# Transformer block on one core: the last four x tiles prepared later, two weight-sum sets moved into the first MLP product, rounds of h's turn every 80 steps

## The chip, the cores and the metric

The kernel runs on one core of one Trainium2 chip. The metric is the device time of one execution in microseconds (us). Lower is better. A run of the kernel also leaves a profile: one execution taken by the hardware profiler, with the records of TensorE (PE, with its weight loads PEld), VectorE (DVE), ScalarE (ACT), GpSimd (POOL), and of SyncE (SP), which issues most of the DMAs.

## The reference

One block: layer norm, an attention with a linear kernel (Hedgehog feature map), a product with `wo`, a residual; then layer norm, an MLP with ReLU, a residual. All in fp32, S = 2048 rows, D = 1024, 32 heads of 32, Dff = 3584.

```python
qkv = layernorm(x) @ wqkv                      # three parts, 32 heads of 32
pq, pk = q @ w_phi, k @ w_phi                  # per head, 32 x 32
phi_q = concat(softmax(pq), softmax(-pq)); phi_k likewise
kv = phi_k^T v;  z = sum of phi_k over the rows
o = (phi_q kv) / (phi_q z + 1e-6)
h = x + o @ wo
out = h + relu(layernorm(h) @ w1) @ w2
```

## The kernel before

**The products.** Each fp32 matrix is split in a high half (rounded to the TensorE type fp32r) and a low half (the rest), and each block of 128 x 128 by 512 takes three matmuls, high x high, high x low and low x high (lines 181, 182 and 183). Such a group of three is a *step*, and the whole kernel is written as a list of steps. A step's place in the list sets the order of instructions on TensorE. Items of eight steps (a tile of 128 rows by a slab of weights) make the projections, items of four steps make the two MLP products.

**The stages, in steps.** K and V for rows 0 to 1023 in four slabs of eight row tiles (steps 0 to 255), Q for these rows in two slabs (256 to 383), then K and V (384 to 639) and Q (640 to 767) for rows 1024 to 2047, the attention, the product with `wo`, the first MLP product (from program step 1024, called `up0`; it starts at 804 us and ends at 1342 us) and the second (to the end). Both MLP products use a scheme of seven instead of eight block products, numbered 1 to 7 and taken in the order 1, 5, 6, 2, 7, 3, 4, so sums of blocks of the weights and of the normalised h are formed beforehand. The first product runs twice over 14 chunks of Dff, once for rows 0 to 1023 (b = 0) and once for the others (b = 1, from 1071 us).

**Everything else is put beside the steps by hand.** `when(step, f, args)` puts a call of `f` behind the matmuls of that step. The calls issue instructions on DVE, ACT, POOL and SP in that order; each engine runs its own instructions in order, and waits in a queue where an operand or a buffer is not there yet. SP issues nearly all loads and stores, in the order of the program, so a load or store that has to wait holds up all DMAs behind it.

**Weights.** `Units.advance`, called behind every step, takes the blocks of weights in the order of their use: it issues the load of a raw block (line 215 and others; six buffers named `raw`) as soon as one of them is free, and a few steps ahead of use it splits the block, the high half by a copy on ACT (line 124), the low half by a subtraction on DVE or POOL (line 128), into a ring of ten buffers named `w`. A raw block's buffer comes free when its low half is done.

**Folded weights.** The feature map's matrix `w_phi` is multiplied into the Q and K weights on the chip. `wt_load` (line 320) loads rows of the transposed weights, `fold_part` (line 335, on TensorE, 64 small matmuls in the group of a fold) multiplies them into the banks, `fold_turn` (line 355, on DVE) transposes the result, `fold_store` (SP) writes it to DRAM, from where it comes back as raw blocks of the K and Q weights (`wpk`, `wpq`). Folds 1 to 7 stand at items 3, 9, 13, 17, 21, 25 and 29.

**The x tiles.** x has 16 tiles of 128 rows. Each of tiles 1 to 6 has steps of its own in `X_STEPS` (load, statistics, power, normalisation, two halves of the transposition). Tiles 0 to 7 go the straight way: load, statistics on DVE (line 221), power on POOL, normalisation on ACT (line 244), transposition on TensorE (line 288) and split. Tiles 8 to 15 are needed only from item 48 on. `X_EARLY` gives each of them a load (line 215), statistics and a normalisation (`xn_norm`, two calls on ACT, two steps apart), after which `xn_store` writes the result to DRAM. Later `xn_load` (line 262) fetches it, 88 to 64 steps ahead (tiles 8 to 11, at steps 241, 257, 273 and 289) or 36 steps ahead (tiles 12 to 15) of the place that `turn` names for its transposition on DVE. The loads of x tiles and of normalised tiles, among others, share the two buffers named `xin` of the pool `lnp`.

**Weight sums.** The sums of blocks of w1 and w2 for the MLP products are made in 56 *sets*, one after another: `t_load` (0.5 MB), four `t_sum` on POOL (line 420) and `t_store` (0.5 MB), written to DRAM and read from there in the MLP stages. `places` is the list of the steps at which they start: the first are the 21 *far* sets in the K and V slabs of the first half, then sets in the Q items and in the second half, and 14 in the first MLP product, from `up0 + 440`, every 25 steps.

**h's turn.** The normalised second half of h is prepared for the first MLP product's second pass in four rounds during its first pass. A round is the list `TURNS`, relative to its start: two reads of h, statistics, two loads of h in another order, normalisation by ACT, two transpositions by DVE (steps 47 and 51), sums on DVE and POOL (52 to 54, line 888), followed by seven stores (`turn_store`, steps 56 to 62). Four rounds start at `up0 + 25 + 84 * i`. Afterwards `h_load` (line 916) fetches each of the seven combinations in two halves, `h_high` (line 924, ACT) makes its high half and `h_low` (line 928, DVE) its low half, in the buffers `hT`, each in its place behind the last product of the first pass that uses the buffer. For b = 0 the low half stands two steps behind the high half for the first four combinations (j < 4) and five steps for the others.

**Beside the first MLP product** `UP_BESIDE` takes each finished bank: `up_take` on ACT (line 957 among them), `up_sum` on DVE (line 954) and so on.

Of the kernel before, what the change touches and what calls it, by code (L numbers as in the profile page):

```python
# [25 lines left out]
NP = NC // 2  # L26
# [113 lines left out]
def kernel(  # L140
# [47 lines left out]
    def do(n, k, f, *args):  # L188
        at[n, k].append((f, args))
# [847 lines left out]
    def item(gen, *args, keys):  # L1037
        items.append((gen, args + (keys,)))
        steps.extend((k,) for k in keys)
        return len(items) - 1  # L1040
# [11 lines left out]
    for b, tiles in enumerate(groups):  # L1052
        for hf in range(2):

            pairs = b == 0 and hf == 0
            for j in range(0, 4, 2 if pairs else 1):
# [3 lines left out]
                for half in range(2):  # L1060
                    n = item(wo_pair, tiles[j:j + 2], hf, half, keys=[("wo", hf, 4 * half + k // 2) for k in range(8)])
# [18 lines left out]
    def x_part(t):  # L1080
        return [x[t * P:(t + 1) * P, :]]
# [6 lines left out]
    def when(step, f, *args):  # L1088

        if step < 8 * first_up:  # L1090
            do(step // 8, step % 8, f, *args)
        else:
            do(first_up + (step - 8 * first_up) // 4, step % 4, f, *args)


    X_STEPS = {1: (None, None, None, None, 5, 7), 2: (None, 6, 8, 10, 12, 13), 3: (None, 10, 11, 14, 18, 20),
               4: (9, 19, 20, 24, 27, 28), 5: (15, 25, 26, 29, 35, 38), 6: (25, 33, 35, 37, 41, 44)}
    X_EARLY = ((48, 74, 86), (64, 84, 98), (88, 102, 112), (100, 115, 138), (116, 140, 154), (142, 158, 170),
               (158, 174, 203), (174, 204, 218))
    for t in range(1, NT):  # L1100
        n = t - 1 if t < HT else q_n[1, t - HT] + 1
        turn = 8 * n + 1
# [2 lines left out]
        else:  # L1105

            load_, stats, norm = X_EARLY[t - HT]
            when(load_, ln_load, ("s", t), x_part(t))
# [22 lines left out]
    for p, n in zip(range(1, 8), (3, 9, 13, 17, 21, 25, 29)):  # L1131
        step = 8 * n + (4 if p > 1 else 7)
# [82 lines left out]
    for u in range(32):  # L1215
        start = 8 * (a0 + u) if u >= 8 else 8 * (last_kv + 4) + 19 * u // 2
        slack = 6 if u < 5 else 0
        if u % 2:
            places = (-8 if u < 12 else -1, 6, 10, 13, 16, 19, 25 if u < 16 else 23)
            when(start + 30 + slack, at_num, u - 1)  # L1220
            when(start + 32 + slack, at_low, u - 1)
        elif u < 16:
            places = (-8 if u < 12 else -1, 6, 10, 13, 16, 19, 25)
        else:
            places = (6, 12, 17, 19, 21, 23, 29)
# [28 lines left out]
    up0 = 8 * first_up  # L1254
    for i in range(4):
        for stage in (0, 1, 2, 3, 9, 4, 5, 6, 7, 8):
            when(wo0 + 64 + 40 * i + LN2[i % 2][stage], ln_pair, 0, i, stage)
        for step, *what in TURNS:
            when(up0 + 25 + 84 * i + step, turn_pair, i, *what)
        for j in range(7):  # L1260
            when(wo0 + 64 + 40 * i + LN2[i % 2][10] + j // 2, ln_store, 0, i, j)
            when(up0 + 25 + 84 * i + 56 + j, turn_store, i, j)
    assert wo_n[8, 0] + 10 < first_up

    def up_step(b, p, m):

        return up0 + 4 * (up_n[b, p, m] + 1 - first_up)

    for j, m in enumerate(UP):

        for g in range(2):
            step = up0 + (8 * j + (-62, -32)[g] if j < 4 else 6 * (j - 4) + 10 + 2 * g)
            high = up0 + (8 * j + (-48, -19)[g] if j < 4 else 6 * (j - 4) + 20 + 2 * g)
            when(step, h_load, 0, m, g)
            when(high, h_high, m, g)
            when(high + (2 if j < 4 else 5), h_low, m, g)
            step = up_step(0, NP - 1, m) + 3 * j
            when(step + 3 * g, h_load, 1, m, g)
            when(step + 18 + 4 * g, h_high, m, g)
            when(step + 21 + 4 * g, h_low, m, g)  # L1280
# [8 lines left out]


    sets = [(w, p, j) for w in (1, 2) for p in range(NP) for j in range(2)]
    places = [64 * q + step for q in range(4) for step in (-9, -1, 7, 15, 23, 31) if 64 * q + step > 9]
    far_sets = len(places)
    places += [264, 274, 284, 294, 314, 364, 374]
    slabs = [8 * kv_n[1, q, HT] for q in range(4)]
    places += sorted([slab + step for slab in slabs for step in (8, 20, 32)] + [slab - 3 for slab in slabs[1:3]])
    places += [up0 + 440 + 25 * n for n in range(14)]
    for n, (step, (w, p, j)) in enumerate(zip(places, sets, strict=True)):
        far = n < far_sets
        when(step, t_load, w, p, j, lnp if step > up0 else fp if far and n % 4 > 1 else tsp)  # L1300
# [4 lines left out]
    for b in range(2):  # L1305
        for m in DOWN:
            n = down_n[b, m, NP - 1] + 1
# [164 lines left out]
```

## Time and profile before

| | |
|---|---|
| time of the runs, median of 3 | 1879.9 us (1879.06 to 1880.86) |
| the profiled execution, its own time | 1880.66 us |
| its span in the profile | 1878.9 us |
| mean granted TensorE clock | 0.998 |
| busy: PE, PEld | 99%, 81% of the span |
| busy: DVE, ACT, POOL | 57%, 40%, 53% |
| DMA traffic | 441.64 MB, mean 235 GB/s |

"Busy" is the time in which an engine executes; the time between two instructions of it counts as idle, and the profile names the instruction on another engine (or the transfer) that ended that idle time. A time of a group of instructions ("L181 PE MATMUL mm<-w") is for the source line 181 of the kernel, with the tile that is written and the tiles that are read. In the rows of a timeline the first number is the start in us from the start of the span, the second the duration, then the engine (SPq is SP's queue of DMAs), the line, the operation, the tiles and, in brackets, how long the engine stood idle just before and for what. The 1.8 us between the profiled execution's own time and its span lie outside the span.

### The profile page before, as it was taken

The page shows a single profiled execution, that of the slowest core. Times are in us where ns is not written, and L with a number is a line of the kernel's source. Part 1 is how long each engine was busy: PE and PEld are TensorE (multiplying, and loading weights), DVE is VectorE, ACT ScalarE, POOL GpSimd, SP SyncE. Part 2 cuts the span into 40 slices and gives each one's busy share as a digit, 9 for nine tenths or more (in the row PEclk, how much of TensorE's full clock was granted, in tenths as well). Part 3 has the DMA queues.
Part 4 walks back from the last instruction along what each step waited for, and adds up shares of the span by engine and source line. Part 5 has one row for each costly group of instructions (what it writes and reads, how often), then busy time and mean ns, then how long its engine had stood idle before and what let it go on. Part 6 is the DMA issues. An engine that isn't in the chain of part 4 may idle for free.

```text
span 1878.9 us, 31761 instructions
## 1 busy us (share of the span) xinstructions
PE 1861.3 (99%) x11502; PEld 1527.8 (81%) x11502; DVE 1074.5 (57%) x1714; ACT 747.1 (40%) x1272; POOL 996.0 (53%) x956
## 2 busy tenths in 40 slices
PE   9999999999999999999999999999999999999999
PEld 7777888888887888888888878888888888888887
DVE  7877789677889676465554674444433333343333
ACT  5443334222233122355454554444444444444442
POOL 4767756678745888233332334435444444444443
PEclk9999999999999999999999999999999999999999
DMA  6799877445465666898687997877877677767775
GB/s 215 245 308 327 291 243 241 131 149 175 135 224 184 206 213 215 266 292 294 214 286 247 297 316 240 264 249 259 274 237 216 205 227 240 236 215 219 216 214 178
DMA packets 320492, 441.64 MB, mean 235 GB/s; under 512 B 28112, under 2 KB 182736, under 8 KB 320336
## 3 DMA queue, kind: packets, MB, share of 16 engines
q1 hardware_dynamic: 291168, 398.69, 66.4%
q10 hardware_dynamic: 29168, 40.93, 6.6%
q8 instruction: 90, 1.47, 0.3%
q14 instruction: 66, 0.54, 0.1%
HBM read 297.96 MB, written 141.57 MB: 234 GB/s over the span
## 4 chain that ended last, share of the span: by engine, by line
PE 88%; DMA 5%; DVE 2%; SPq 1%; issue 1%; ACT 1%; POOL 1%; DVEq 0%; ACTq 0%; POOLq 0%
PE mm L181 22%; PE mm L182 22%; PE mm L183 22%; PE ac L183 3%; PE ac L182 3%; PE ac L181 3%; PE tp L181 2%; PE tp L183 2%; PE tp L182 2%; DMA hT<-hs 1%; PE tp L720 1%; PE ac L533 1%; PE ac L720 1%; DMA raw<-in_w_dram 1%; PE tp L288 1%
## 5 line engine op out<-in xcount | busy, mean ns | idle before, releaser
L128 POOL TENSOR_TENSOR w<-raw,w 128x512 fp32r<-128x512 f32 x353 | 476.5, 1352 | 641.7 <-ACT w L124 619.6
L124 ACT ACTIVATE w<-raw 128x512 fp32r<-128x512 f32 x686 | 408.9, 626 | 485.0 <-PE mm L183 221.1
L128 DVE TENSOR_TENSOR w<-raw,w 128x512 fp32r<-128x512 f32 x333 | 279.4, 840 | 508.8 <-ACT w L124 503.0
L181 PE MATMUL mm<-w,xT 128*128 128x512 f32 x752 | 298.3, 397 | 2.9 <-ACT w L124 2.9
L182 PE MATMUL mm<-w,xT 128*128 128x512 f32 x752 | 293.4, 390 | 0.5 <-POOL w L128 0.2
L183 PE MATMUL mm<-w,xT 128*128 128x512 f32 x752 | 292.8, 389 | 0.0
L182 PE MATMUL mm<-hT,w 128*128 128x512 f32 x672 | 261.8, 390 | 2.8 <-DVE hT L928 2.8
L181 PE MATMUL mm<-hT,w 128*128 128x512 f32 x672 | 261.6, 389 | 0.7 <-DVE c L954 0.7
L183 PE MATMUL mm<-hT,w 128*128 128x512 f32 x672 | 261.4, 389 | 0.0
L420 POOL TENSOR_TENSOR b<-b 128x256 f32<-128x256 f32 x168 | 133.4, 794 | 78.5 <-DMA b<-in_w_dram 70.0
L181 PEld LDWEIGHTS mm<-w,xT 128*128 128x128 f32 x752 | 141.3, 188 | 35.1 <-ACT w L124 3.3
L182 PEld LDWEIGHTS mm<-w,xT 128*128 128x128 f32 x752 | 141.4, 188 | 31.0 <-POOL w L128 1.1
L183 PEld LDWEIGHTS mm<-w,xT 128*128 128x128 f32 x752 | 141.3, 188 | 29.8
L181 PE MATMUL mm<-w 128*128 128x512 f32 x392 | 152.5, 389 | 0.0
L182 PE MATMUL mm<-w 128*128 128x512 f32 x392 | 152.5, 389 | 0.0
L183 PE MATMUL mm<-w 128*128 128x512 f32 x392 | 152.5, 389 | 0.0
L182 PEld LDWEIGHTS mm<-hT,w 128*128 128x128 f32 x672 | 126.1, 188 | 30.2 <-DVE hT L928 4.1
L181 PEld LDWEIGHTS mm<-hT,w 128*128 128x128 f32 x672 | 126.1, 188 | 27.4 <-DVE c L954 1.1
L183 PEld LDWEIGHTS mm<-hT,w 128*128 128x128 f32 x672 | 126.2, 188 | 25.9
L522 POOL TENSOR_TENSOR zacc<-zacc,kphi 128x512 f32<-128x512 f32 x60 | 82.7, 1378 | 7.0 <-DVE kphi L514 7.0
L181 PEld LDWEIGHTS mm<-w 128*128 128x128 f32 x392 | 73.6, 188 | 15.3
L183 PEld LDWEIGHTS mm<-w 128*128 128x128 f32 x392 | 73.6, 188 | 15.3
(200 smaller groups left out, 3181.0 us busy)
## 6 DMA issues: line engine op xcount, KB each, us to landing
raw<-t SPq DMA_DIRECT2D x224, 256.0 KB, 4.3
raw<-ad SPq DMA_DIRECT2D x196, 256.0 KB, 3.0
raw<-in_w_dram SPq DMA_DIRECT2D x168, 256.0 KB, 3.4
ad<-c SPq DMA_DIRECT2D x112, 256.0 KB, 4.2
b<-in_w_dram SPq DMA_DIRECT2D x42, 512.0 KB, 5.6
t<-b SPq DMA_DIRECT2D x42, 512.0 KB, 3.9
ad<-s SPq DMA_DIRECT2D x84, 256.0 KB, 4.7
ed<-qe ACTq DMA_DIRECT2D x32, 512.0 KB, 4.3
```

Of the source, the lines that this page charges most:

```text
L124: nc.scalar.activation(w[:, 0, :], raw[1], AF.Copy)
L128: eng.tensor_tensor(out=w[:, 1, :], in0=raw[1], in1=w[:, 0, :].bitcast(F32), op=ALU.subtract)
L181: pe.matmul(ps, a_hi, b_hi, start=first, stop=False, skip_group_check=more)
L182: pe.matmul(ps, a_hi, b_lo, start=False, stop=False, skip_group_check=more)
L183: pe.matmul(ps, a_lo, b_hi, start=False, stop=last, skip_group_check=more)
L288: pe.transpose(pt[:, k, :], xn[:, (4 * j + k) * P:(4 * j + k + 1) * P], ident)
L420: pool.tensor_tensor(out=tsum[j, *out], in0=tsum[j, *a], in1=tsum[j, *b], op=ALU.subtract)
L522: pool.tensor_tensor(out=zacc[s], in0=zacc[s], in1=phi_of[key], op=ALU.add)
L533: pe.matmul(kv_ps[s][g][32 * i:32 * (i + 1), 0:64], vt[:, 32 * h:32 * (h + 1)], phi[:, 64 * h:64 * (h + 1)], start=first, stop=last)
L720: pe.matmul(banks[g][32 * c:32 * (c + 1), r * P:(r + 1) * P], kvL[rows, 4 * q + 2 * sd + h // 4, 32 * (h % 4):32 * (h % 4 + 1)], phT[rows, ...
```

## The change

It edits six lists of steps, and no instruction's shape or kind.

- **x tile 6.** Statistics, power and normalisation at steps 30, 33 and 36, before at 33, 35 and 37.
- **x tiles 12 to 15, early pass.** The loads at steps 140, 168, 206 and 232 (before 116, 142, 158 and 174), the statistics and the normalisation, and with it the store, 14 to 36 steps behind their loads as listed below.
- **Far sets.** `places` now leaves out steps 119 and 183. The number of far sets falls from 21 to 19. As the sets are made in a fixed order, each set takes the next place in the list.
- **Sets in the first MLP product.** 16 of them, every 22 steps, from the same step; before 14, every 25 steps.
- **h's turn.** Rounds every 80 steps, with their stores; before every 84.
- **h_low for j >= 4 (b = 0)** stands three steps behind `h_high`, before five. **h_load for b = 1** stands `5 * j // 2` steps behind the last product of the first pass, before `3 * j`; `h_high` and `h_low` move with it.

```diff
-               4: (9, 19, 20, 24, 27, 28), 5: (15, 25, 26, 29, 35, 38), 6: (25, 33, 35, 37, 41, 44)}
-    X_EARLY = ((48, 74, 86), (64, 84, 98), (88, 102, 112), (100, 115, 138), (116, 140, 154), (142, 158, 170),
-               (158, 174, 203), (174, 204, 218))
+               4: (9, 19, 20, 24, 27, 28), 5: (15, 25, 26, 29, 35, 38), 6: (25, 30, 33, 36, 41, 44)}
+    X_EARLY = ((48, 74, 86), (64, 84, 98), (88, 102, 112), (100, 115, 138), (140, 154, 166), (168, 182, 203),
+               (206, 220, 230), (232, 246, 268))
...
-            when(up0 + 25 + 84 * i + step, turn_pair, i, *what)
+            when(up0 + 25 + 80 * i + step, turn_pair, i, *what)
...
-            when(up0 + 25 + 84 * i + 56 + j, turn_store, i, j)
+            when(up0 + 25 + 80 * i + 56 + j, turn_store, i, j)
...
-            when(high + (2 if j < 4 else 5), h_low, m, g)
-            step = up_step(0, NP - 1, m) + 3 * j
+            when(high + (2 if j < 4 else 3), h_low, m, g)
+            step = up_step(0, NP - 1, m) + 5 * j // 2
...
-    places = [64 * q + step for q in range(4) for step in (-9, -1, 7, 15, 23, 31) if 64 * q + step > 9]
+    places = [64 * q + step for q in range(4) for step in (-9, -1, 7, 15, 23, 31) if 64 * q + step not in (-9, -1, 7, 119, 183)]
...
-    places += [up0 + 440 + 25 * n for n in range(14)]
+    places += [up0 + 440 + 22 * n for n in range(16)]
```

The three numbers of an entry of `X_EARLY` are the steps of the load, the statistics and the normalisation of one tile, for tiles 8 to 15 in order.

## The prediction, made before the changed kernel ran

> **What bounds the kernel now.** I read the page's busy times first, then TensorE's own waits, then the short windows around each wait, then the queue that fed it.
>
> ```profile
> PE 1861.3 (99%) x11502; PEld 1527.8 (81%) x11502; DVE 1074.5 (57%) x1714; ACT 747.1 (40%) x1272; POOL 996.0 (53%) x956
> ```
>
> TensorE (PE) is busy 99% of the span, and the change adds and removes no matmul. So only PE's idle time and its slow-clock time can move. The view of waits, for PE alone:
>
> ```profile
> PE mm L181 <- ACT w L124: 2.9, 1, 2.9
> PE mm L182 <- DVE hT L928: 2.8, 3, 1.3
> PE tp L335 <- DMA wt<-in_wqkT_dram: 2.5, 2, 2.3
> ```
>
> ```profile
> PE mm L181 <- DVE c L954: 0.7, 1, 0.7
> PE tp L288 <- ACT xn L244: 0.4, 1, 0.4
> ```
>
> These five rows are what the change can reach. Rows one and three are single gaps at 122 and 155 us, in the first K/V projections; rows two and four lie in the first MLP product, at 826, 1069, 1100 and 1107 us; the last is at 50 us. The windows of 4 us around the first two gaps (columns: PE, PEld, DVE, ACT, POOL busy, granted clock, DMA share, GB/s):
>
> ```profile
> 120.00:124.00 4.00, 2.58 (x12) 1.81 (x10) 0.38 (x1) 0.00 (x0) 2.77 (x2) 1.00 0.89 253
> 124.00:128.00 4.00, 2.31 (x9) 1.67 (x10) 2.02 (x5) 1.34 (x3) 1.57 (x3) 1.00 1.04 355
> 128.00:132.00 4.00, 4.00 (x94) 2.70 (x96) 3.64 (x9) 2.34 (x5) 2.66 (x3) 1.00 1.08 382
> ```
>
> ```profile
> 156.00:160.00 4.00, 2.63 (x92) 1.41 (x96) 0.00 (x0) 1.36 (x2) 3.69 (x5) 0.82 1.06 385
> 160.00:164.00 4.00, 4.00 (x59) 3.36 (x52) 2.71 (x7) 0.08 (x1) 0.00 (x0) 0.75 1.07 391
> ```
>
> The transfers are full here (share about 1), while other engines idle: the gaps are late loads, not late arithmetic. After the second gap the granted clock falls: 4 x 0.18 + 4 x 0.25 = 1.7 us of full-speed work lost.
>
> **The change, part by part.** A "step" is three matmuls, 0.68 us (the windows of 16 us below hold 72 matmuls each); within an engine the order of the trace is the order of the code, so each row can be given its step.
>
> *Gap at 122 us (step 135).* PE waits for the last weight block of slab 2. In the queue of SyncE (SP):
>
> ```profile
> 118.58 0.39 SPq L215 DMA_DIRECT2D xin<-in_x_dram  x1
> ...
> 130.38 0.33 SPq L376 DMA_DIRECT2D raw<-wpk  x1
> ```
>
> ```profile
> 119.55 5.14 DMA raw<-in_wv_dram
> ```
>
> The second fence is a row of the chain: the block was issued at 119.55 and took 5.14 us. Just ahead of it stands the load of x tile 12 (0.5 MB, step 116), which the change moves to step 140. Without it the block is issued about 0.5 us sooner and has 0.524 MB less ahead of it: 1.5 us at the 355 GB/s of the second window, 2.1 at the 253 of the first. The bounds are nothing and the whole 2.9; I take 1.8, as those rows are the nearest. The set moved away from step 119 stood behind the block and does not help here.
>
> *Gap at 155 us (step 172).* PE waits for the rows that it folds. SP issued them at 149.75, thirteen steps after the code's place for them (step 152), and they needed 7.6 us:
>
> ```profile
> 149.75 0.98 SPq L320 DMA_DIRECT2D wt<-in_wqkT_dram  x2
> ```
>
> ```profile
> wt<-in_wqkT_dram SPq DMA_DIRECT2D x2, 512.0 KB, 7.6
> ```
>
> Ahead of them go, after the change: x tile 12's load (step 116), and the set of step 119, a load, four sums on POOL and a store. Tile 13's load of step 142 is replaced by tile 12's at 140. That is 1.57 MB, 4.2 us at the 370 GB/s between the windows' 355 and 385. The set's sums also leave POOL, which SP waits for before each store:
>
> ```profile
> L420 POOL TENSOR_TENSOR b<-b 128x256 f32<-128x256 f32 x168 | 133.4, 794 | 78.5 <-DMA b<-in_w_dram 70.0
> ```
>
> 4 x 0.79 = 3.2 us. And the long wait of SP before 130.38, for a store of folded weights that has these two loads (1.05 MB) ahead of it, ends some 2.7 us sooner at 385 GB/s. The rows thus come about 4 us earlier (bounds 1.5 and 7), while PE wants them 1.8 earlier: 2.3 + 1.8 = 4.1 us is needed, so the gap closes to about nothing. I count 2.3 plus the restart of 0.16 that the rows at 826 us below show, 2.5. With the gap goes the slow clock, 1.7. What is late next is the block of step 196; the set of step 183 no longer stands in POOL's way, and I count nothing for it.
>
> *Statistics of x tile 6, step 33 to 30.* They now run ahead of the eight transposes of the fold instead of behind them:
>
> ```profile
> 41.99 1.44 DVE L355 STREAM_TRANSPOSE wp<-mm 128x256 f32<-128x256 f32 x4
> 43.35 1.40 DVE L355 STREAM_TRANSPOSE wp<-tp 128x256 f32<-128x256 f32 x4
> ...
> 45.98 1.27 DVE L221 BATCH_NORM_STATS2 st<-xin 128x6 f32<-128x512 f32 x2
> ```
>
> ```profile
> 44.70 0.60 PE L288 MATMUL tp<-ident,xn 128*128 128x128 f32 x4
> ...
> 50.30 0.66 PE L288 MATMUL tp<-ident,xn 128*128 128x128 f32 x4 [0.40 <-ACT xn L244]
> ```
>
> The normalisation then comes early enough for 50.30: 0.4 and restart saved. But PE's transposes at 44.70 write the first of two tp banks, which half of the second row frees at about 44.1. Shifted by 1.3 us of statistics this is 45.4: a new wait of 0.7 and restart. Net a loss of 0.3 (bounds: a gain of 0.6, if the statistics find an idle place, and a loss of 1).
>
> *Low halves of h, five steps after the high ones to three (gap at 826 us).*
>
> ```profile
> 823.82 0.69 DVE L128 TENSOR_TENSOR w<-raw,w 128x512 fp32r<-128x512 f32 x1 [7.40 <-ACT w L124]
> 824.43 2.35 DVE L928 TENSOR_TENSOR hT<-hT 128x1024 fp32r<-128x1024 f32 x2
> ```
>
> ```profile
> 818.64 1.06 ACT L924 ACTIVATE hT<-hT 128x1024 fp32r<-128x1024 f32 x1 [0.17 <-DMA hT<-hs]
> ```
>
> ```profile
> 825.75 0.39 PE L181 MATMUL mm<-hT,w 128*128 128x512 f32 x1
> 826.84 0.50 PE L182 MATMUL mm<-hT,w 128*128 128x512 f32 x1 [0.70 <-DVE hT L928]
> ```
>
> The first low half was ready to run at 819.7, but stood behind a weight split that waited 7.40 us. At its new place it runs before it; the second one then ends at 825.7 instead of 826.8, and PE, which would use it at 825.75 + 0.23, no longer waits. The gap goes: 0.70, and 0.16 of restart, since from 825.75 to 826.84 is 1.09 against 0.23 + 0.70.
>
> *Rounds of h's turn every 80 steps (gaps at 1069, 1100, 1107).* The fourth round moves up by 12 steps, 8.2 us:
>
> ```profile
> 1035.27 1.75 POOL L888 TENSOR_TENSOR xin<-xin,s 128x512 f32<-128x512 f32 x1 [4.38 <-ACT c L957]
> ```
>
> ```profile
> 1040.44 0.33 SPq L389 DMA_DIRECT2D raw<-in_w_dram  x1
> ...
> 1052.47 2.54 SPq L916 DMA_DIRECT2D hT<-hs  x4
> ```
>
> ```profile
> 1059.09 1.06 ACT L924 ACTIVATE hT<-hT 128x1024 fp32r<-128x1024 f32 x1 [7.96 <-DMA hT<-hs]
> ```
>
> ```profile
> 1016.00:1032.00 16.00, 16.00 (x72) 13.23 (x71) 5.10 (x7) 9.28 (x18) 5.67 (x7) 1.00 0.52 165
> 1032.00:1048.00 16.00, 16.00 (x73) 13.23 (x72) 14.36 (x16) 7.09 (x15) 8.05 (x5) 1.00 0.63 207
> ```
>
> The round's last sums wait on POOL, the weight splits behind them free their buffers late, SP waits until 1040.44, then issues the round's seven stores and only at 1052.47 the first load of h for the second half, some twenty steps after its place. ACT stands 7.96 us for it. Moved up, the stores (1.8 MB) fall where the share is 0.52 and 0.63, SP is some 8 us less late, and the loads for the last products come two to three steps earlier still (5j//2 for 3j). I count all three gaps gone: with the 826 one 2.8 + 0.7 and 4 x 0.16 of restart, 4.1 (bounds 0 and 4.1).
>
> *At nothing.* Tiles 13 to 15's later norms and stores: nothing reads them before step 325. The two more sets in the first product, every 22 steps: 2 x 3.2 us on POOL and 2 MB, under work that leaves POOL half idle:
>
> ```profile
> 1128.00:1332.00 204.00, 204.00 (x902) 168.98 (x901) 88.71 (x112) 88.82 (x151) 91.51 (x86) 1.00 0.78 254
> ```
>
> *One new wait.* SP's load of turned tile 9 (step 257) takes the buffer that tile 15 now holds until its norm at step 270. Behind it in SP's queue stand the weights of the next Q slab and five sets:
>
> ```profile
> 220.39 1.40 SPq L262 DMA_DIRECT2D xin<-xnd  x1
> 225.15 3.81 SPq L380 DMA_DIRECT2D raw<-wpq  x6
> ```
>
> ACT can run that norm before PE's step 270, so I expect 4 us, at most 9; the weights are used at step 320, 63 steps or 43 us further on. No cost.
>
> **Sum.** -1.8 - 2.5 - 1.7 + 0.3 - 4.1 = -9.8 us against the profiled execution's own 1880.66, 1870.9; the median of the runs, 1879.9, stands 0.8 below that: 1870.1.
>
> **Rivals.** *SP stays paced by POOL's sums* (waits that were hidden come out when the transfers thin): the gap at 155 and its slow clock stay, +4.2, 1874.3. For it: the 70.0 us that those sums wait for their own loads. Against: the loads come earlier too. *The fourth round collides:* its second transpose on DVE (step 316 of the product) now stands ahead of the sum that frees a bank for step 328, at about 1028 us; with the round 8.2 us earlier I find some 1.5 us of slack. If its data are later than that, PE waits there and ACT, DVE and SP fall behind as before: +4.1, 1874.2. *The slow clock is the fold's own,* its 64 small matmuls, not the gap's: 1.7 stays, 1871.8. Against it, the window 128 to 132 holds such a fold at clock 1.00. The Trainium skill (TensorE: Matmul & The Clock Gate, Part 1: The HAM clock gate) has half clock follow an idle window of about 3.4 us; by that rule a gap of 2.3 us would not halve it, and the sum would be -8.1. The trace has the fall right behind the gap, so I go by the row. *No change:* each gap closed opens the next one, 1877 to 1881. *Slower:* SP's hold at step 257. Each of the five sets behind it makes a round trip of load, sum and store on POOL and SP; if the hold lasts over 12 us past 225, the splits from step 313 on come late, and PE waits one us for each further one, six blocks in a row. It decides only where the hold passes 20 us: 1884 and up. ACT's norm would have to be that late, which nothing before it shows.
>
> **Chances.** The forecast 0.49, slow clock kept 0.08, POOL pacing 0.11, collision 0.10, no change 0.13, slower 0.09. What this kernel's measurement can tell from no change is about 0.2%, 3.8 us: faster than 1876.1 0.78, within 0.13, slower 0.09. The forecast's own range is 1867 (first gap wholly gone, no new wait at 45 us) to 1872.5; the range for all reaches over the two partial cases, 1866.5 to 1877.5.
>
> **What would show it.** In the waits of PE: no row for L335 on wt, none for L928 and c; the row of L181 on ACT near 1 us; a new one for L288 near 45 us, on DVE. Clock 1.00 from 100 us to the end. ACT's wait for hT near 1059 gone, the DMA share in 1016 to 1048 higher. A gap of over 1 us at 1028, or any at 260 to 275, would make the prediction wrong.

## The result, and the profile after

The changed kernel took 1867.85 us (median of 6 runs, 1866.56 to 1871.89) against 1881.14 us of the kernel before on the same chip: a ratio of 0.9934, 95% interval 0.992 to 0.9947. On another chip it took 1868.05 against 1881.37, 0.993 (0.9917 to 0.9942). That is about 13 us, where the forecast was 9.8. The time lies in the stated range, and the sign and the places were right; one step of the sum, the second gap, worked out in another way than it was told.

Two profiled executions of the changed kernel are shown, because they differ where the forecast was most in doubt. The first was the slowest of its runs (span 1870.1 us), the second (span 1866.2 us) near the median. The waits of TensorE in the first, in the order in which the view gives them (total us, times, longest):

```profile
PE tp L335 <- DMA wt<-in_wqkT_dram: 2.6, 2, 2.2
...
PE mm L181 <- ACT w L124: 1.4, 1, 1.4
PE tp L288 <- DVE wp L355: 0.6, 1, 0.6
```

And in the second:

```profile
PE tp L335 <- DMA wt<-in_wqkT_dram: 0.9, 2, 0.8
PE tp L288 <- DVE wp L355: 0.6, 1, 0.6
```

Of the five rows of before, those of L928 and of c are gone in both, as forecast. The wait of L181 on the split weights, 2.9 before, is 1.4 in the first and gone in the second. The wait for the rows of fold 5 is 2.2 in the first, nearly as long as before, and 0.8 in the second. The new wait near 44 us, on VectorE's transposes, is the one that was forecast (0.7).

The windows of 4 us around fold 5 show the granted clock (the column behind POOL's), in the first execution and then in the second:

```profile
152.00:156.00 4.00, 1.43 (x65) 0.75 (x64) 1.41 (x4) 2.19 (x4) 3.77 (x6) 1.00 1.00 341
156.00:160.00 4.00, 4.00 (x94) 3.27 (x70) 1.65 (x5) 0.00 (x0) 1.74 (x2) 0.57 1.11 384
```

```profile
152.00:156.00 4.00, 3.77 (x133) 2.64 (x134) 0.00 (x0) 0.00 (x0) 3.48 (x5) 1.00 1.08 381
156.00:160.00 4.00, 4.00 (x20) 3.29 (x18) 3.78 (x10) 0.38 (x1) 1.15 (x2) 1.00 1.09 394
```

With the long gap the clock falls (0.57), with the short one it stays at 1.00.

These executions issue the same 11502 matmuls in the same order, so the start of each can be set against its start before. The table gives how far TensorE moved across each place, in us, against the profiled execution of before:

| place (time before) | forecast | first execution | second execution |
|---|---|---|---|
| start, up to 13 us | 0 | -1.2 | +0.4 |
| tile 6, 44 to 51 us | +0.3 | +0.2 | +0.2 |
| 73 to 75 us | 0 | -0.3 | -0.3 |
| gap at 122 us | -1.8 | -1.5 | -3.7 |
| gap at 155 us | -2.5 | -0.1 | -1.6 |
| slow clock behind it | -1.7 | +0.2 | -1.6 |
| 177 us | 0 | -0.9 | -0.9 |
| 592 to 706 us | 0 | -0.5 | -0.6 |
| gap at 826 us | -0.9 | -1.0 | -0.9 |
| gaps at 1069, 1100, 1107 us | -3.3 | -3.7 | -3.7 |
| sum | -9.8 | -8.8 | -12.7 |

The first row is not the change's: no edit touches the start, and the last section shows what moves it.

In the first MLP product, the last store of the fourth round and the first loads behind it, the ScalarE copy that stood 7.96 us, and the two windows whose share was 0.52 and 0.63, in the first execution:

```profile
1028.35 0.70 SPq L900 DMA_DIRECT2D hs<-s4l  x1
...
1040.12 2.78 SPq L916 DMA_DIRECT2D hT<-hs  x4
```

```profile
1046.47 1.06 ACT L924 ACTIVATE hT<-hT 128x1024 fp32r<-128x1024 f32 x1 [0.44 <-DMA hT<-hs]
```

```profile
1016.00:1032.00 16.00, 16.00 (x72) 13.26 (x71) 11.37 (x15) 8.28 (x15) 7.31 (x5) 1.00 0.65 216
1032.00:1048.00 16.00, 16.00 (x72) 13.24 (x71) 7.21 (x11) 7.56 (x13) 4.32 (x3) 1.00 1.03 361
```

The first load of h for the second half is issued at 1040.12 where it was 1052.47; TensorE by itself is only some 5 us earlier there. ScalarE's wait fell from 7.96 to 0.44 us, and the transfers now fill the window that they left idle.

### The profile page after: what moved, and what is told of

It is laid out like the page before. It is cut to its first block, busy times and chain, and to the rows that moved or that the text cites. A ratio compares the mean times of both kernels' runs of the same rounds, so it can differ in the third digit from the quotient of the medians.

```text
span 1870.1 us, 31754 instructions
## 1 busy us (share of the span) xinstructions
PE 1858.1 (99%) x11502; PEld 1527.3 (82%) x11502; DVE 1066.5 (57%) x1714; ACT 748.4 (40%) x1272; POOL 992.4 (53%) x956
## 4 chain that ended last, share of the span: by engine, by line
PE 95%; DMA 2%; DVE 1%; SPq 1%; ACT 0%; POOL 0%; issue 0%; ACTq 0%; DVEq 0%; POOLq 0%
PE mm L181 24%; PE mm L182 24%; PE mm L183 24%; PE ac L183 4%; PE ac L182 4%; PE ac L181 4%; PE tp L183 2%; PE tp L182 2%; PE tp L181 2%; PE tp L720 1%; PE ac L533 1%; DMA raw<-in_wv_dram 1%; PE ac L720 1%; PE tp L288 1%; DMA wt<-in_wqkT_dram 0%; DMA b<-in_w_dram 0%
## 5 line engine op out<-in xcount | busy, mean ns | idle before, releaser
L128 POOL TENSOR_TENSOR w<-raw,w 128x512 fp32r<-128x512 f32 x353 | 471.7, 1339 | 637.2 <-ACT w L124 605.5
L128 DVE TENSOR_TENSOR w<-raw,w 128x512 fp32r<-128x512 f32 x333 | 273.2, 821 | 507.3 <-ACT w L124 491.4
L181 PE MATMUL mm<-w,xT 128*128 128x512 f32 x752 | 298.3, 397 | 1.4 <-ACT w L124 1.4
L181 PE MATMUL mm<-hT,w 128*128 128x512 f32 x672 | 261.4, 389 | 0.0
L181 PEld LDWEIGHTS mm<-w,xT 128*128 128x128 f32 x752 | 141.4, 188 | 33.6 <-issue 2.3
L420 POOL TENSOR_TENSOR b<-b 128x256 f32<-128x256 f32 x160 | 126.5, 790 | 76.9 <-DMA b<-in_w_dram 69.1
L181 PE MATMUL mm<-w 128*128 128x512 f32 x392 | 152.5, 389 | 0.0
L181 PEld LDWEIGHTS mm<-hT,w 128*128 128x128 f32 x672 | 126.1, 188 | 26.2
```

Source lines behind the costliest of these rows:

```text
L128: eng.tensor_tensor(out=w[:, 1, :], in0=raw[1], in1=w[:, 0, :].bitcast(F32), op=ALU.subtract)
L181: pe.matmul(ps, a_hi, b_hi, start=first, stop=False, skip_group_check=more)
L420: pool.tensor_tensor(out=tsum[j, *out], in0=tsum[j, *a], in1=tsum[j, *b], op=ALU.subtract)
```

## The experiments

The time of each is against the kernel before on the same chip, whose median was 1880.98 us for the first four, 1881.37 for the next four and 1881.55 for the last three.

| kernel | median us | ratio | 95% interval |
|---|---|---|---|
| part of h alone | 1875.37 | 0.9972 | 0.9961 to 0.9982 |
| the change without it | 1874.03 | 0.9963 | 0.995 to 0.9976 |
| x tiles 12 to 15 alone | 1878.81 | 0.9985 | 0.9974 to 0.9997 |
| sets alone | 1877.08 | 0.9983 | 0.9975 to 0.9991 |
| changed kernel again | 1868.05 | 0.9930 | 0.9917 to 0.9942 |
| tile 6 back | 1870.31 | 0.9939 | 0.9927 to 0.9952 |
| rows of fold 5 earlier | 1866.67 | 0.9921 | 0.9907 to 0.9934 |
| fold 5 issued twice | 1868.30 | 0.9932 | 0.9918 to 0.9945 |
| loads of h back | 1868.16 | 0.9931 | 0.9918 to 0.9945 |
| rounds of h back | 1870.43 | 0.9942 | 0.9929 to 0.9956 |
| rows earlier, two more edits | 1865.97 | 0.9922 | 0.9909 to 0.9936 |

**The part of h alone.**

```diff
 # on the kernel before
-            when(up0 + 25 + 84 * i + step, turn_pair, i, *what)
+            when(up0 + 25 + 80 * i + step, turn_pair, i, *what)
 # turn_store likewise; h_low at high + 3 for j >= 4; h_load at 5 * j // 2
```

> Of the change only the part of h: the rounds every 80 steps, h_low three steps behind h_high, h_load for b = 1 at 5j//2; x tiles and sets as before, 14 sets every 25 steps. Theory (the four gaps at 826, 1069, 1100 and 1107 us are this part's alone): they go, 4.1 us by the prediction's sum, 4.7 by the matched matmuls of the two profiles, so a ratio of 0.9975 to 0.998, and the waits at 122 and 155 us stay as they were (2.9 and 2.3). Rival (the two additional sets and their spacing of 22 steps have to do with it): one of the four gaps stays, ratio 0.9985 or above.

Measured 0.9972, 5.6 us between the medians, of which 4.7 show in the profile: all four gaps are gone. The theory holds for them, and the two additional sets have no part in it. The waits at 122 and 155 us did not stay as they were: they are 3.6 and 1.0 us in this profile, and two more, of 0.9 and 1.7 us, stand at 178 and 181 us on GpSimd's split, all in code that this kernel does not change. The remaining 0.9 us is not placed; the length of the gap at 826 us differs between executions (0.7 before; 0.8, 1.4 and 2.7 in the next three kernels, which keep that code of before).

**The change without the part of h.**

```diff
 # on the changed kernel: the four edits above undone
```

> The change without the part of h: tile 6, the early passes of tiles 12 to 15 and the sets are changed, h's rounds stand at 84 steps with h_low and h_load as before. Theory (the parts add up): the rest of the measured ratio of 0.9934, so 0.9955 to 0.9965 (6.6 to 8.5 us), with the four gaps of h in the trace. Rival (sets every 22 steps collide with rounds every 84): the waits on h in the first MLP product are longer than the 2.8 and 0.7 us of before, ratio above 0.997.

Measured 0.9963, 6.95 us. With the 5.6 of the other part that is 12.6 of the 13.1 to 13.3: the parts add up. Three of the four gaps of h are there, and none is longer than before by more than 0.1 us, so there is no sign that the sets every 22 steps collide with the rounds.

**The x tiles alone, and the sets alone.**

```diff
 # x alone, on the kernel before
+    X_EARLY = (... (140, 154, 166), (168, 182, 203), (206, 220, 230), (232, 246, 268))
 # sets alone, on the kernel before
+    places = [... if 64 * q + step not in (-9, -1, 7, 119, 183)]
+    places += [up0 + 440 + 22 * n for n in range(16)]
```

> Only the early passes of tiles 12 to 15 are later; sets, tile 6 and h as before. Theory (the load of tile 12 was what made the last weight block of slab 2 late): the wait at 122 us shrinks from 2.9 to about 1.4 us, the one at 155 stays at 2 to 2.4, ratio 0.999. Rival (the sets made it late, the load of tile 12 did not): 2.9 us stays, ratio 1.000.

> Only the sets are changed: without the places 119 and 183, 16 every 22 steps in the first MLP product; x tiles and h as before. The wait at 122 us stays at 2.9. Theory of the prediction (the rows of fold 5 are late by the bytes ahead of them): 1.05 MB less, they come some 2.8 us sooner, while TensorE wants them at the same time, so the wait at 155 us goes and with it the slow clock, 4.2 us, and the short wait at 177 us, 0.8: ratio 0.9973. Rival (SyncE's queue is paced by GpSimd's sums, by the folded weights' store and by its own issues, and what is taken out of it is filled): the wait at 155 stays at 2 us or more, and only the 0.8 us at 177 is gained: ratio 0.9995.

TensorE's waits in the kernel with the x tiles alone, and then in that with the sets alone:

```profile
PE tp L335 <- DMA wt<-in_wqkT_dram: 3.3, 1, 3.3
...
PE mm L181 <- ACT w L124: 1.3, 1, 1.3
```

```profile
PE mm L182 <- DVE hT L928: 4.3, 3, 2.7
PE mm L181 <- ACT w L124: 3.5, 1, 3.5
...
PE mm L182 <- POOL w L128: 0.7, 1, 0.7
```

Each cures one gap and worsens or leaves the other. Without tile 12's load the first gap is 1.3; the second grows to 3.3, because TensorE arrives 1.6 us earlier and the rows only 0.7, counted from the start of fold 3. Without the two sets the first gap is 3.5, with a slow clock behind it, but the second is gone: no row of L335 is left, and the rows come 3.5 us earlier. Gains of 2.2 and 3.9 us against 1.9 and 5.0 expected. So what the two sets put ahead of the rows did decide, and the rival that SyncE is paced in any case falls for the sets. A set is bytes, sums on GpSimd and issues of SyncE at once; which of them held the rows up, as the prediction had it by the bytes, this run cannot tell. The 0.8 us at 177 us was not gained: TensorE waits 0.7 us there for GpSimd's split, 0.2 before. The kernel with the x tiles alone gains 0.7 us there. The wait of 2.7 on h in the second list is the gap at 826 us, in code that this kernel does not change.

What sets the length of the first gap shows in all thirteen profiles. Counted from the start of fold 3, TensorE wants the last block of slab 2 at 19.7 us, and in each profile the wait is the time by which its landing comes later than that. Three kernels load tile 12 at step 116: before, h alone and sets alone. There the block lands at 22.5, 23.3 and 23.2 us, its transfer takes 5.1 to 5.3 us, and TensorE stands 2.9, 3.6 and 3.5 us. In the ten other profiles it lands at 17.5 to 21.1 us, its transfer takes 3.0 to 4.7 us, the wait is 1.4 us at the most, and in six of them there is none for ScalarE's split.

**The changed kernel a second time.**

> The changed kernel itself, a second time, for another profile beside those of the next three kernels. Theory (the first profiled execution, 1871.89 us, was one of the minority in which fold 5 waits some 2 us and the clock falls; the runs at a mean clock of 1.000 have neither): ratio 0.993 again, and a profiled execution with a mean clock of 1.000 shows a wait at 152 us of under 1 us and a clock of 1.00 there. Rival (the gap is there in all runs): a profiled execution at 1.000 with a wait of 2 us or more at 152 us.

Measured 0.993; the profiled execution, the second of the table above, has the clock 1.000, a wait of 0.8 us and no fall. The theory holds for this execution. In the eleven timed executions of the changed kernel the mean clock was 1.000 in nine and 0.999 in the two slowest of the first set, 1870.97 and 1871.89 us.

**Tile 6 back.**

```diff
-               ... 6: (25, 30, 33, 36, 41, 44)}
+               ... 6: (25, 33, 35, 37, 41, 44)}
```

> The changed kernel with tile 6's statistics, power and normalisation back at steps 33, 35 and 37. Theory (the change of tile 6 trades a wait of 0.40 us at 50 us for one of 0.62 at 44): the wait on DVE near 44 us goes, the one on ACT near 50 us comes back, 0.2 us less in all, which no run can show; ratio 0.993 as the changed kernel. Rival (the earlier statistics let the following folds and splits run earlier, as matmuls from 51 to 75 us gained 0.3 us more in two profiles): 0.3 to 0.5 us lost, ratio 0.9935.

Measured 0.9939, 2.3 us above the changed kernel, the intervals overlapping. In the profile the new wait near 44 us is gone, the old one is back:

```profile
PE tp L288 <- ACT xn L244: 0.4, 1, 0.4
```

Set against the second execution TensorE gains 0.8 us at 46 us, loses 0.6 at 51 and 0.4 at 74. The last is the rival's: against before, every profile with the edit moves 0.3 to 0.4 us earlier there, and those without it 0.1 to 0.8 later; by what way was not followed. So the edit gains some 0.2 us or more over the whole stretch where the sum had a loss of 0.3; the rest of the 2.3 lies between executions (a wait of 0.4 at 121 us and one of 0.6 at 818 us in this profile) and is not shown to be due to tile 6.

**The rows of fold 5 one item earlier.**

```diff
 # on the changed kernel
-        do(max(n - 2, 1), 0, wt_load, p, sp)
+        do(max(n - (3 if p == 5 else 2), 1), 0, wt_load, p, sp)
```

> The changed kernel with the load of fold 5's rows one item (8 steps, 5.4 us) earlier in SyncE's queue, at step 144. Theory (what was missing is place in the queue, not bytes): the rows land 4 to 7 us earlier, the wait at 152 us is gone in every run, the clock stays at 1.00 there, 0 to 4.5 us less than the changed kernel by whether the run had the gap; ratio to before 0.992. Rival (the rows then delay the weight blocks behind them): the gap turns into one of matmuls of line 181 on ACT between 128 and 160 us, ratio 0.994 or more.

Measured 0.9921, all five runs between 1865.47 and 1867.14 us and at a clock of 1.000. The issue of the rows, in the queue of SyncE:

```profile
138.75 1.56 SPq L320 DMA_DIRECT2D wt<-in_wqkT_dram  x2
```

That is some 8 us earlier than in the first execution of the changed kernel (146.83), where TensorE is 2 us later. The rows are there 3 us ahead of fold 5, and no wait of L335 is left, nor any other between 50 and 580 us. The theory holds for the gap, though the gain of 1.4 us over the changed kernel lies within the intervals. Another wait is there: 0.7 us at 817 us on a low half of h, the place of the gap at 826 us before, in code that this edit does not touch. Of all kernels tried this is the one to keep. What was left of the second gap was place in the queue.

**Fold 5 issued twice.**

```diff
 # on the kernel with the rows earlier; the output is the same
-        for i in range(2):
+        for i in (0, 1, 0, 1) if p == 5 else range(2):
```

> As the kernel with the rows earlier, and the 64 small matmuls of fold 5 are issued twice into the same banks (the second time over the first), so that there is low activity on TensorE without a wait. They take some 2.4 us once. Theory (the clock falls where too little of the array is busy for long enough, and small matmuls count as idle): without a wait at 152 us the clock behind the fold falls to between 0.6 and 0.85 in 4 us, and the time is 2.4 + about 1.7 us above the kernel with the rows earlier. Rival (only idle time counts): the clock stays at 1.00 behind the fold, 2.4 us more.

Windows of this kernel around the doubled fold:

```profile
148.00:152.00 4.00, 4.00 (x136) 2.79 (x134) 1.42 (x4) 2.13 (x3) 3.35 (x5) 1.00 1.09 380
152.00:156.00 4.00, 4.00 (x94) 3.24 (x77) 2.78 (x7) 0.38 (x1) 2.90 (x4) 1.00 0.83 278
```

128 small matmuls and the 64 of `kv_third` behind them, 3.8 us from 149.5 to 153.3, with no wait ahead: the clock stays at 1.00. So these small matmuls alone do not make it fall; behind each fall of the thirteen traces that is read below stands idle time. The median is 1.6 us above the kernel it was made from; one run of four was at 0.999. The doubled fold took 1.3 us more, not 2.4: the expectation had mis-sized it.

**h's loads back at 3j, and h's rounds back at 84,** each on the changed kernel.

```diff
-            step = up_step(0, NP - 1, m) + 5 * j // 2
+            step = up_step(0, NP - 1, m) + 3 * j
 # and, in the other kernel
-            when(up0 + 25 + 80 * i + step, turn_pair, i, *what)
+            when(up0 + 25 + 84 * i + step, turn_pair, i, *what)
```

> The changed kernel with the loads of h for b = 1 (and the high and low halves behind them) back at 3j steps; rounds at 80. Theory of the prediction (the fourth round, moved up by 12 steps, frees SyncE's queue for the loads, the 5j//2 adds two to three steps of margin): the gap on c near 1062 us stays gone, those on h's low halves near 1091 and 1097 us come back in part, at most 1.4 of their 2.7 us; ratio 0.993 to 0.994. Rival (the earlier places of the loads close them alone): both come back in full, 2.7 us, ratio 0.9945.

> The changed kernel with h's rounds, and their stores, back at every 84 steps; loads of h at 5j//2. Theory of the prediction (the fourth round sets how late SyncE is): the gaps near 1062, 1091 and 1097 us come back, 3.0 to 3.7 us, ratio 0.995; ScalarE again waits about 8 us for h near 1052. Rival (the places of the loads decide): only the gap on c near 1062 comes back, 0.3 to 1.0 us, ratio 0.9935.

With the loads back no gap on h returns and the ratio is 0.9931: that edit brought nothing that can be seen. With the rounds back it is 0.9942, 2.3 us above the other kernel on the same chip; TensorE's waits and ScalarE's copy in that kernel:

```profile
PE mm L182 <- DVE hT L928: 1.4, 1, 1.4
...
PE ac L182 <- DVE hT L928: 0.6, 1, 0.6
```

```profile
1049.16 1.06 ACT L924 ACTIVATE hT<-hT 128x1024 fp32r<-128x1024 f32 x1 [8.01 <-DMA hT<-hs]
```

ScalarE's wait of 8 us is back, and two gaps on h with it, one in a new place (1079 us), which cost 2.9 us against the other kernel. Only the gap on c is not. So the fourth round sets how late the loads are, as the prediction had it, and neither theory was right for c.

**Two more edits for the waits that were left,** on the kernel with the rows earlier.

```diff
-        fold_turn(p, (2, 3))
-        if p == 1:
-            fold_turn(p, (0, 1))
+        if p == 1:
+            fold_turn(p, (0, 1))
+        fold_turn(p, (2, 3))
...
-            step = up0 + (... 6 * (j - 4) + 10 + 2 * g)
+            step = up0 + (... 6 * (j - 4) + 6 + 2 * g)
```

> The kernel with the rows of fold 5 earlier, and two more edits for the waits that the profiles of the changed kernel still show: in fold 1 the two banks that TensorE's transposes need next (heads 0 and 1) are transposed by VectorE ahead of the others, and h's loads for j >= 4 of the first pass stand four steps earlier. Theory: the wait of L288 near 44 us (0.62) and that of L182 on h near 816 us (0 to 0.8) go, 0.8 to 1.8 us with their restarts less than the kernel with the rows earlier (0.9921): 0.9914. Rival (the other two banks then hold up the next products, or the loads of h those of the weights): a wait of the same size on mm banks or weights, ratio 0.992.

Both waits are gone from its profile, but one of 0.7 us on the weights stood at 120 us, one of 0.3 at 307, and one run of five fell to a clock of 0.998 (1870.31 us). Ratio 0.9922: no gain over the rows alone can be shown.

## Why the prediction was right, and where not

*The gap at 122 us.* Right in cause: the load of tile 12 made the block late. The term of 1.8 measured 1.5 and 3.7 in the two executions, the larger with a short wait beside it. The transfer was foreseen well: the prediction took 1.5 to 2.1 us off its 5.14, and it was 1.3 and 2.2 shorter. The issue was not: counted from the start of fold 3 it came 0.2 us sooner in the first execution and 2.9 in the second, where the prediction had 0.5. So the upper bound, the whole wait of 2.9, was nearer for the second.

*The gap at 155 us.* The step that did not work out is "2.3 + 1.8 = 4.1 us is needed, so the gap closes to about nothing". Six profiles have the changed x tiles and sets and the rows' load in its place (the two executions, the change without h, tile 6 back, loads of h back and rounds of h back). In all but the first execution the rows land 4.2 to 5.4 us earlier, counted from the start of fold 3, so "about 4 us earlier" held; but TensorE wants them 2.5 to 3.7 earlier, not 1.8, and a wait of 0.3 to 1.0 us is left. The step had fixed what TensorE wants by its size of the first gap; the more of that gap closes, the less is gained here. In the first execution the rows come only 1.6 us earlier, TensorE 1.5, and 2.2 us are left. SyncE was late there well ahead of the rows: 2.7 us later than in the second execution at the block of the first gap, 2.8 at the rows. Why was not followed. The rival "SP stays paced by POOL's sums" has this execution's numbers near its own (2.2 us left, and 1871.9 against the 1874.3 that it gave), but the sets alone close the gap by themselves and the rows earlier close it too, so its mechanism is not shown.

*The slow clock.* Right for these two executions: it goes where the gap goes. That it is the fold's own, its small matmuls without a wait, falls with the doubled fold. But a short gap is no safety: in the change without h waits of 1.0 and 0.5 us at fold 5 had a fall behind them.

*Tile 6.* The new wait near 44 us was foreseen to 0.1 us. The gain of 0.3 at 73 us was not.

*Counted at nothing.* At 177 us 0.9 us were gained that the sum does not have. The view of waits had a row for it:

```profile
PE mm L182 <- POOL w L128: 0.2, 1, 0.2
```

The prediction named the set of step 183 there and counted nothing for it. The set by itself does not close it: with the sets alone the wait is 0.7 us, while with the later x tiles alone it is gone. But it differs between profiles of the same code there (0.9 and 1.7 with h alone, as before; 0.5 with the loads of h back, as in the changed kernel), so what closes it is not shown. No cost came from the other pieces counted at nothing, nor from the hold of SyncE at step 257: TensorE shows no wait between 260 and 275 us, nor at 1028.

*h.* Right in cause and near in size, 4.1 against 4.7 and 4.6, as the restarts were counted at 0.16 and measured 0.3. That the earlier loads for b = 1 add to it was not shown. The gap at 826 us is closed less surely than the other three: a wait of 0.2 to 0.7 us stands in its place in the profiles of three other kernels that have the edit (tile 6 back, rows earlier, fold 5 twice).

*The sum.* The terms came to 9.8; the second execution, whose own time is near the median, stands 12.7 below. The first gap's 1.9, the 0.9 at 177 us, 0.4 on h, 0.3 at 73 and 0.1 at tile 6 are 3.6 more than the terms, the 0.9 that the second gap brought less and 0.1 of the clock are 1.0 less; some 0.2 lies in places that no edit touches (0.6 at 592 to 706 us, against 0.4 at the start), and the rest is rounding. The further half microsecond between the medians is not placed. In the first execution, the slowest of its six, 8.8 us show, of which 1.2 lie at the start.

## What to carry to other kernels

Two waits in a row on one transfer queue are not two terms of a sum: closing the first moves up the time at which the second transfer is wanted, so each edit has to be tried against the other's place, as the x tiles alone (second gap 2.3 to 3.3) showed. Where the bytes ahead of a late transfer are already reduced, asking for it one item earlier removed what was left, at no cost that the medians show. One profiled execution is one draw: a gap of 2.2 us in it was 0.8 in the next of the same kernel, so the medians and further profiles decide which is typical.

## What the runs showed of the hardware

The clock fell without a fold too. In the kernel with the sets alone TensorE stood 2.65 us at 822 us, among full matmuls only:

```profile
821.98:825.39 3.41, 0.82 (x4) 0.36 (x2) 2.96 (x4) 3.31 (x5) 0.75 (x1) 1.00 1.09 339
825.39:828.80 3.41, 3.35 (x8) 2.70 (x9) 3.41 (x6) 2.22 (x4) 1.14 (x1) 0.50 1.06 330
```

Over the profiles, waits of 3.3, 3.5 and 3.6 us were followed by a slow clock each time, of 1.9 to 2.9 us six times out of seven (three of them at 6 to 8 us, in the start of the kernel; the 2.9 at 122 us before was not), and of 1.7 us or less not, but for one of 1.0 and one of 0.5 us on either half of fold 5 in the change without the part of h. So it is not the length of a wait alone.

The record of the granted clock in the traces shows what else counts. Each slow piece inside the kernels lasts 3.41 us, and two of one trace start a whole number of such pieces apart: at 8.37 and 158.56 us before (44 pieces), at 125.66 and 825.39 us with the sets alone (205). If a trace is cut into these pieces, the one just ahead of each of the ten falls holds 1.5 to 3.4 us in which TensorE is idle. The wait of 2.9 us before lies across two pieces, with 1.8 us (3.41 less the 1.57 busy) in one and 1.3 in the other, and no fall follows:

```profile
121.01:124.42 3.41, 1.57 (x7) 0.95 (x6) 0.00 (x0) 0.00 (x0) 1.76 (x2) 1.00 0.88 296
124.42:127.84 3.42, 2.15 (x8) 1.55 (x9) 2.02 (x5) 1.18 (x3) 1.48 (x2) 1.00 1.02 354
```

Over 2 us of idle time in one piece were followed by a fall each time, under 1.5 us never. In between it went both ways: 1.8 us among full matmuls had none, 1.5 and 1.8 beside the small matmuls of fold 5 had one. Whether small matmuls count in part as idle is not shown; 3.0 us of them in one piece, in the doubled fold, had no fall.

The Trainium skill (TensorE: Matmul & The Clock Gate, Part 1: The HAM clock gate) has the clock drop after an idle window of about 3.4 us and lets that window run freely. The runs agree on the length of the piece, and that a wait of the same length falls or not by where it lies; they differ on the idle time, since 1.5 to 2.6 us inside one piece were enough.

One slow piece costs 1.7 us and lowers the mean clock of an execution by 0.0009. The mean clock does not tell where: the start of the kernel, which no edit touches, differed by up to 1.9 us between profiled executions. Before, with h alone and without h the clock falls there, from 8 us on, behind a wait of 1.9 to 2.2 us. In the second execution of the changed kernel the record begins only at 11.1 us, and the profile counts 10 matmuls between 8 and 10 us, against 19 in the first. In the nine other profiles the wait is 1.1 to 1.7 us and no fall follows.
